# Attention and gated feed-forward in one kernel: norm statistics on half the columns, a finer weave in the first batch, and an earlier load

## The chip, the cores and the metric

The kernel runs on one core of a Trainium2 chip. The metric is the device time of one execution in microseconds (us), taken as the median of several runs. The engines named below are TensorE (PE in the profile; its weight loads are PEld), VectorE (DVE), ScalarE (ACT), GpSimd (POOL) and SyncE (SP); the last two issue most of the transfers (DMAs).

## The reference

There are 8 batches, 12 heads, 448 tokens and 64 numbers per head; the feed-forward has 768 inputs (12 x 64) and 1536 hidden units.

```python
scores = q @ k.T / sqrt(64)                    # per batch and head, 448 x 448
attn   = maximum(scores, 0)**2 / 448
x      = attn @ v                              # heads side by side: 3584 tokens x 768
rms    = sqrt(mean(x*x, axis=-1) + 1e-6)       # one number for each token
xn     = x / rms * rms_g
g, val = xn @ w_gate, xn @ w_val
out    = (g / (1 + exp(-g)) * val) @ w_out     # 3584 x 768, float32
```

## The kernel before

Everything is kept transposed: features on the partitions, a batch's 448 tokens along the columns. `xT` holds the attention's output of a batch as 6 blocks of 128 features (two heads each), `xD` the same with the halves of the partitions exchanged, made by four `swap` DMAs on SP's queue (L292). With both, each gate and value product contracts over 64 rows at a time, and two matmuls run side by side on the upper and lower rows. One round of `rounds` (L447) is such a pair, for gate (`psG`) and for value (`psV`); a block of 128 hidden units takes 12 rounds, the first 6 on `xT`, the last 6 on `xD`. Then ACT takes the silu of `psG` (L499) and DVE multiplies it by `psV` (L501) into `hT`. `outproj` (L505) multiplies `hT` by `w_out`, and ACT copies the result (`psO`) out (L521) for the stores (L532).

The order of instructions on every engine is the order in which the Python code emits them. `weave(main, sides)` emits a list of main units (half blocks of gate work, then output tiles), and ahead of main unit n every side step whose position is at most n. The side steps of batch b's gate are the attention of batch b+1. `along(p0, gap, fns)` gives such positions.

Attention of a pair of heads in batch 1 (`attention_second`, L326): `pe_transposes` turns k and q by TensorE into `psT`, and ACT or DVE copies them to `qkT`; a visit, `pair_scores` (L190), makes the scores of one of four groups of keys with two matmuls into `psS`, and ACT (L207), or DVE for the fourth group (L205), takes the relu; `squares` (L240, multiplying at L246) runs on DVE; `values` emits `attend` (L251, 16 matmuls into `psAV`) and `leave` (L275), in which ACT makes two blocks of `xT` (L284) and the squares `x2` (L285). `psS` and `psAV` share two buffers (pool `ps_s`); `psT`, `psG`, `psV`, `psO` share four (pool `ps_m`, tag "mm"). A matmul into a buffer waits until its former content has been read.

Batch 0 comes first, its attention alone (`attention_first`). Then the first EB = 3 blocks of batch 0's gate run on the raw `xT` and `xD`, before the norm is known, into `psE`; `early_out` copies them (L467), and `early_scale` (L473, DVE) and `early_rest` (L480 on ACT, L482 on DVE) finish them later. The other nine blocks of batch 0, with the attention of batch 1 woven in (`attention_second`; four of its steps have been taken by then), are the stage that the diff touches at the end: L652 to L658. From batch 2 on attention is `attention(b)` (L353), on halves of transposes made by DMA (`transposes`, L146, on SP; `fill`, L163, on GpSimd).

`norm_stat(b)` makes 1/rms of a batch: a matrix of ones, times the squares `x2`, gives every partition the sum over features (`psSS`); ACT takes the root, a further small ACT instruction brings back the table of silu, and DVE takes the reciprocal (`rstd`), which `norm_apply` (L425) multiplies onto `xT` block by block (L435), with a `swap` after three blocks and after six. For batches 0, 1 and 7 it takes 12 matmuls of 448 columns. For batches 2 to 6 `norm_stat_split` takes 6: the lower partitions get the sum of the even blocks and the upper ones that of the odd blocks, which a copy and an addition then bring together. For batch 1 it is emitted ahead of the first output tile, later after the first half of one.

GpSimd's queue loads in the order of emission (L582 to L607): batch 0, slices 0 and 1 of the gate and value weights (256 hidden units each), q and k of batch 1 in halves of six heads, slices 2 and 3, v of batch 1, slices 4 and 5, then `w_out`. `fetch(b)` loads a later batch.

Of the kernel before, what the change touches and what calls it, by code (L numbers as in the profile page):

```python
# [8 lines left out]
FP32 = mybir.dt.float32  # L9
BF16 = mybir.dt.bfloat16  # L10
ALU = mybir.AluOpType
ACT = mybir.ActivationFunctionType
# [22 lines left out]
def kernel(  # L35
# [20 lines left out]
    eps = 1e-6  # L56
    inv_attn = 1.0 / (float(D) * float(S))
    NT = 2 * S // P
    HALF = P // 2

    ctx.enter_context(tc.manual_schedule())

# [21 lines left out]
    def alloc_ld(b):  # L84
        for nm in ("q", "k", "v"):
            ld[nm, b] = ldpool.tile([PC, H, NCH * D], BF16, name=nm + "b", tag=nm + "b", bufs=2)
# [153 lines left out]
    def squares(b, j, cs, split=False):  # L240
        r = raw.pop((b, j, cs[0]))
        if split:
            nc.scalar.activation(out=r[:, 0], in_=r[:, 0], func=ACT.Square)
            nc.vector.tensor_tensor(out=r[:, 1], in0=r[:, 1], in1=r[:, 1], op=ALU.mult)
        else:
            nc.vector.tensor_tensor(out=r[:], in0=r[:], in1=r[:], op=ALU.mult)  # L246
        for i, c in enumerate(cs):
            for hh in range(2):
                rsq[b, 2 * j + hh, c] = r[:, i, hh, :]
# [76 lines left out]
    def attention_second(b):  # L326

        steps = []

        def visit(j, c):  # L330
            pair_scores(b, j, c, c == 3 and j > 0)
            if c == 0 and j:
                squares(b, j - 1, (2, 3))
            if c == 2:
                squares(b, j, (0, 1))

        def values(j):
            attend(b, (j, j + 1))
            leave(b, (j, j + 1))

        for j in range(HP):
            for c in range(NCH):
                steps.append(lambda j=j, c=c: visit(j, c))
                if c == 3 and j + 2 < HP:
                    steps.append(lambda j=j: pe_transposes(b, j + 2))
                if c == 3 and j in (2, 4):
                    steps.append(lambda j=j: values(j - 2))
        steps.append(lambda: squares(b, HP - 1, (2, 3)))
        steps.append(lambda: None)
        steps.append(lambda: values(HP - 2))  # L350
        return steps
# [29 lines left out]
    def halves(ps, w, lhsT, rhs, start, stop):  # L381

        for hf in range(2):
            prt = slice(hf * HALF, (hf + 1) * HALF)
            nc.tensor.matmul(out=ps[prt, :w], lhsT=lhsT[:, prt], rhs=rhs, start=start, stop=stop)  # L385

    def norm_stat(b):
        if 1 < b < B - 1:
            return norm_stat_split(b)
        psSS = ps_s.tile([P, 2, 512], FP32, name="psSS", tag="psS")[:, 0, :S]  # L390
        rstd = npool.tile([P, S], FP32, name="rstd", tag="rstd")
        for kt in range(KT):
            halves(psSS, S, ones_bf, x2s[b][:, kt, :], kt == 0, kt == KT - 1)
        nc.scalar.activation(
            out=rstd[:], in_=psSS[:], func=ACT.Sqrt, scale=1.0 / float(DM), bias=eps_col[:]
        )
        nc.scalar.activation(out=warm_act[:], in_=eps_col[:], func=ACT.Silu)
        nc.vector.reciprocal(out=rstd[:], in_=rstd[:])
        rstds[b] = rstd

    def norm_stat_split(b):


        psSS = ps_m.tile([P, S], FP32, name="psSS", tag="mm")
        rstd = npool.tile([P, S], FP32, name="rstd", tag="rstd")
        for i in range(KT // 2):
            for hf in (0, 1):
                prt = slice(HALF * hf, HALF * (hf + 1))
                nc.tensor.matmul(
                    out=psSS[prt, :], lhsT=ones_bf[:, prt], rhs=x2s[b][:, 2 * i + hf, :],  # L410
                    start=(i == 0), stop=(i == KT // 2 - 1),
                )
        low, high = slice(0, HALF), slice(HALF, P)
        nc.scalar.copy(out=rstd[low, :], in_=psSS[high, :])
        nc.vector.tensor_tensor(out=rstd[low, :], in0=psSS[low, :], in1=rstd[low, :], op=ALU.add)
        for prt in (high, low):
            nc.scalar.activation(
                out=rstd[prt, :], in_=rstd[low, :], func=ACT.Sqrt, scale=1.0 / float(DM),
                bias=eps_col[prt, :],
            )  # L420
        nc.scalar.activation(out=warm_act[:], in_=eps_col[:], func=ACT.Silu)
        nc.vector.reciprocal(out=rstd[:], in_=rstd[:])
        rstds[b] = rstd

    def norm_apply(b):  # L425
# [21 lines left out]
    def rounds(b, fb, parts, r0, r1, x=None):  # L447

        for r in range(r0, r1):
            kt, own = r % KT, r < KT  # L450
            src = (x or (xTs[b], xDs[b]))[0 if own else 1]
            for part in range(2):
                prt = slice(part * HALF, (part + 1) * HALF)
                h = 2 * kt + (part if own else 1 - part)
                nc.tensor.matmul(  # L455
                    out=parts[part][:, :S],
                    lhsT=wgv_sb[prt, h, fb * P : (fb + 1) * P],
                    rhs=src[prt, kt, :],
                    start=(r == 0),
                    stop=(r == 2 * KT - 1),  # L460
                )
# [24 lines left out]
    early = {}  # L486
    gvs = {}

    def block_first(b, fb):
        gvs[b, fb] = [  # L490
            ps_m.tile([P, S], FP32, name=nm, tag="mm")[:] for nm in ("psG", "psV")
        ]
        rounds(b, fb, gvs[b, fb], 0, KT)

    def block_second(b, fb):
        psG, psV = gvs.pop((b, fb))
        rounds(b, fb, (psG, psV), KT, 2 * KT)
        s = spool.tile([P, S], BF16, name="sil", tag="sil")
        nc.scalar.activation(out=s[:], in_=psG, func=ACT.Silu)  # L499
        hT, o = hidden(b)  # L500
        nc.vector.tensor_tensor(out=hT[:, fb, o : o + S], in0=s[:], in1=psV, op=ALU.mult)  # L501
# [33 lines left out]
            )  # L535
            g, k = g + n, k + 1

    def gate_value(b, f0=0):
        units = []
        for fb in range(f0, FT):  # L540
            units.append(lambda fb=fb: block_first(b, fb))
            units.append(lambda fb=fb: block_second(b, fb))
        if b < B:
            units[1], units[2] = units[2], units[1]
        return units

    def out_tiles(i, t0, t1):
# [41 lines left out]
    def warm(n):  # L589

        ps = ps_m.tile([P, S], FP32, name="psW", tag="mm")
        for _ in range(n):
            nc.tensor.matmul(out=ps[:], lhsT=warm_in[:, :P], rhs=warm_in[:], start=True, stop=True)  # L593

    for s in range(2):
        fetch_gv(s)
    alloc_ld(1)
    for h0 in (0, HH):
        load("q", 1, h0, h0 + HH)
        load("k", 1, h0, h0 + HH)  # L600
    for s in range(2, 4):
        fetch_gv(s)
    load("v", 1)
# [11 lines left out]
    with tc.tile_pool(name="qkT", bufs=2, side="right") as tp, tc.tile_pool(  # L615
        name="early", bufs=EB, side="right"
    ) as ep:
        late["qkT"], late["early"] = tp, ep
        warm(12)
        steps = attention_second(1)  # L620
        first = attention_first(0)
        for n, fn in enumerate(first):
            if n == len(first) - 3:
                pe_transposes(1, 0)
            if n == len(first) - 1:
                pe_transposes(1, 1)
            fn()
            if n % 3 == 2:
                warm(2)
        def early_block(fb):  # L630
            return [ps_m.tile([P, S], FP32, name="psE", tag="mm")[:] for _ in range(2)]

        raw_x = xTs[0], xDs[0]
        blocks = [early_block(fb) for fb in range(2)]
        near, far = KT + 4, 2 * KT
        norm_stat(0)
        rounds(0, 0, blocks[0], 0, KT, raw_x)
        rounds(0, 1, blocks[1], 0, KT, raw_x)
        for fb in range(2):
            steps.pop(0)()  # L640
            rounds(0, fb, blocks[fb], KT, near, raw_x)
        norm_apply(0)
        for fb in range(2):
            rounds(0, fb, blocks[fb], near, far, raw_x)
            early_out(0, fb, blocks[fb])
        for fb in range(2, EB):
            blocks.append(early_block(fb))
            for r0 in range(0, far, KT):
                steps.pop(0)()
                rounds(0, fb, blocks[fb], r0, r0 + KT, raw_x)  # L650
            early_out(0, fb, blocks[fb])
        main = gate_value(0, EB)  # L652
        sides = along(3.2, 1, [lambda fb=fb: early_scale(0, fb) for fb in range(EB)])
        sides += along(5.2, 1, [lambda fb=fb: early_rest(0, fb) for fb in range(EB)])
        sides += along(0, (len(main) - 1) / len(steps), steps)
        sides += [(9.1, lambda: fetch(2))]
        sides += [(14, lambda: trans_fill(2, 0)), (16, lambda: trans_fill(2, 1))]
        weave(main, sides)  # L658
    late["ost"] = pool("ostage", 3)

# [55 lines left out]
```

## Time and profile before

| | us |
|---|---|
| median of 12 runs (455.62 to 457.57) | 456.75 |
| the profiled execution | 456.38 |
| its span, first to last instruction | 454.6 |
| PE busy | 441.5 (97%) |
| ACT busy | 285.5 (63%) |
| DVE busy | 271.9 (60%) |
| DMA on GpSimd's queue, share of 16 engines | 41.9% |
| granted TensorE clock | 0.999 |

A row of a group or of the timeline gives line, engine, operation, result <- operands, form (partitions x columns) and count; in the timeline the start and the duration stand ahead, and in brackets behind stands how long the engine had been idle and what ended that. In a group's row the busy time, the mean duration of one in nanoseconds and the idle time before it follow. A row of the windows gives, for a stretch of time, its length, the busy time of PE, PEld, DVE, ACT and POOL (number of instructions in brackets), the clock, the DMA engines' share and GB/s. The ends of matmuls are modelled, so a busy PE is not a PE at its peak.

### The profile page before, as it was taken

How to read it: one execution, taken by the hardware profiler on the slowest of the kernel's cores; microseconds unless marked ns; L12 is line 12 of the kernel's file. 1: busy time of each engine (PE TensorE's matmuls, PEld its weight loads, DVE VectorE, ACT ScalarE, POOL GpSimd, SP SyncE). 2: the span in 40 equal slices, each digit the busy share in tenths (PEclk: the TensorE clock that was granted, in tenths of full speed). 3: DMA queues.
4: the chain of work that ended last, by engine and by line, in shares of the span. 5: the costliest groups of instructions: out<-in, count | busy, mean ns of one | idle time of the engine just before them, and what ended most of it. 6: DMA issues, size and time to landing. Idle time of an engine off the chain costs nothing.

```text
span 454.6 us, 10811 instructions
## 1 busy us (share of the span) xinstructions
PE 441.5 (97%) x4718; PEld 248.0 (55%) x4718; DVE 271.9 (60%) x326; ACT 285.5 (63%) x425; POOL 53.5 (12%) x79
## 2 busy tenths in 40 slices
PE   7999989999999999999999999999999999999996
PEld 3444444755556555555556555655556555565664
DVE  4979885637746666376656566386755466452210
ACT  4888786567766676676757577576757576542221
POOL 8333210400000300003000300003000000000000
PEclk9999999999999999999999999999999999999999
DMA  9999999997004998069913998059911910041013
GB/s 135 200 207 204 200 205 157 180 266 128 1 1 114 182 194 80 1 147 196 158 32 74 198 195 101 1 126 200 175 32 39 211 45 1 1 120 47 1 37 106
DMA packets 86672, 53.44 MB, mean 118 GB/s; under 512 B 36576, under 2 KB 80480, under 8 KB 86624
## 3 DMA queue, kind: packets, MB, share of 16 engines
q0 software_dynamic: 44496, 27.50, 41.9%
q1 hardware_dynamic: 41632, 24.67, 28.2%
q8 instruction: 37, 0.61, 0.5%
q10 hardware_dynamic: 496, 0.57, 0.4%
q14 instruction: 11, 0.09, 0.1%
HBM read 47.19 MB, written 11.01 MB: 128 GB/s over the span
## 4 chain that ended last, share of the span: by engine, by line
PE 84%; ACT 6%; DMA 4%; DVE 3%; issue 1%; SPq 1%; DVEq 0%
PE psG L455 35%; PE psO L385 20%; PE psV L455 9%; PE psAV L263 8%; PE psS L218 6%; DMA xD<-xT 4%; PE psW L593 2%; ACT r L187 1%; DVE xT L435 1%; PE psS L177 1%; ACT r L207 1%; PE psT L134 1%; SPq L292 1%; ACT xT L284 1%; ACT x L285 1%
## 5 line engine op out<-in xcount | busy, mean ns | idle before, releaser
L455 PEld LDWEIGHTS <-wgv_sb 64*128 64x128 bf16 x2304 | 122.0, 94 | 97.5 <-issue 10.4
L455 PE MATMUL psV<-xD,wgv_sb 64*128 64x448 bf16 x558 | 120.6, 349 | 0.9 <-DMA xD<-xT 0.8
L455 PE MATMUL psG<-xD,wgv_sb 64*128 64x448 bf16 x558 | 120.8, 349 | 0.0
L455 PE MATMUL psG<-xT,wgv_sb 64*128 64x448 bf16 x558 | 120.6, 349 | 0.0
L455 PE MATMUL psV<-xT,wgv_sb 64*128 64x448 bf16 x558 | 120.4, 349 | 0.0
L501 DVE TENSOR_TENSOR hT<-sil,psV 128x448 bf16<-128x448 bf16 x93 | 57.6, 619 | 104.9 <-ACT sil L499 103.9
L385 PE MATMUL psO<-wo_sb,hT 128*64 128x512 bf16 (+1 forms) x1344 | 113.5, 326 | 0.0
L232 ACT ACTIVATE r<-psS 112x896 bf16<-112x896 f32 x108 | 96.2, 918 | 22.7 <-PE psS L218 22.7
L385 PEld LDWEIGHTS <-hT 128*64 128x64 bf16 x1344 | 74.9, 110 | 36.2 <-issue 4.1
L499 ACT ACTIVATE sil<-psG 128x448 bf16<-128x448 f32 x93 | 50.7, 545 | 59.0 <-PE psV L455 38.9
L236 DVE TENSOR_TENSOR r<-r 112x1792 bf16<-112x1792 bf16 x72 | 78.3, 1089 | 4.9 <-ACT r L232 3.9
L521 ACT COPY ost<-psO 128x512 f32<-128x512 f32 (+1 forms) x54 | 25.2, 482 | 39.3 <-PE psO L385 35.0
L218 PE MATMUL psS<-qT,kT 64*128 64x448 bf16 (+1 forms) x288 | 47.8, 351 | 0.3 <-DVE r L230 0.3
L284 ACT ACTIVATE xT<-psAV,ga_sb 128x448 bf16<-128x448 f32 x47 | 27.5, 631 | 26.4 <-PE psAV L263 26.4
L230 DVE TENSOR_SCALAR r<-psS 112x896 bf16<-112x896 f32 x36 | 39.0, 1083 | 5.0 <-PE psS L218 5.0
L263 PE MATMUL psAV<-r,vb 112*64 112x448 bf16 x384 | 41.5, 356 | 0.0
L165 POOL DMA_DIRECT2D qT<-qT x12 | 6.5, 539 | 272.1 <-PE psS L218 143.8
L263 PEld LDWEIGHTS <-vb 112*64 112x64 bf16 x384 | 19.5, 109 | 19.8 <-issue 8.7
L218 PEld LDWEIGHTS <-kT 64*128 64x128 bf16 (+1 forms) x288 | 17.2, 96 | 19.3 <-issue 8.2
L435 DVE TENSOR_TENSOR xT<-xT,rstd 128x448 bf16<-128x448 bf16 x48 | 26.4, 619 | 0.3
L246 DVE TENSOR_TENSOR r<-r 112x1792 bf16<-112x1792 bf16 x23 | 24.4, 1084 | 1.3 <-ACT r L207 1.2
L285 ACT ACTIVATE x<-psAV 128x896 bf16<-128x896 f32 (+1 forms) x27 | 22.6, 836 | 0.8 <-DVE xT L280 0.8
(65 smaller groups left out, 254.7 us busy)
## 6 DMA issues: line engine op xcount, KB each, us to landing
vb<-in_v_dram POOLq DMA_DIRECT2D x7, 672.0 KB, 18.6
xD<-xT SPq DMA_DIRECT2D x28, 168.0 KB, 2.7
qb<-in_q_dram POOLq DMA_DIRECT2D x6, 672.0 KB, 12.4
kb<-in_k_dram POOLq DMA_DIRECT2D x6, 672.0 KB, 15.4
qT<-qT POOLq DMA_DIRECT2D x24, 168.0 KB, 3.7
out_dram<-ost SPq DMA_DIRECT2D x7, 336.0 KB, 5.8
wgv_sb<-in_moe_w_gate_dram POOLq DMA_DIRECT2D x6, 384.0 KB, 16.4
wgv_sb<-in_moe_w_val_dram POOLq DMA_DIRECT2D x6, 384.0 KB, 17.2
```

Of the source, the lines that this page charges most:

```text
L218: nc.tensor.matmul(out=psS[: end - o, hf, :S], lhsT=flat[prt, o:end], rhs=qT[prt, 1 - hf : 3 - hf, h % HH], start=True, stop=True,)
L230: nc.vector.tensor_relu(out=r[:, cp], in_=src)
L232: nc.scalar.activation(out=r[:, cp], in_=src, func=ACT.Relu)
L236: nc.vector.tensor_tensor(out=r[:], in0=r[:], in1=r[:], op=ALU.mult)
L263: nc.tensor.matmul(out=part[hh * D : (hh + 1) * D, :], lhsT=ld["v", b][:, 2 * j + hh, c * D : (c + 1) * D], rhs=rsq[b, 2 * j + hh, c], sta ...
L284: nc.scalar.mul(out=xTs[b][:, j, :], in_=psAV[:, i, :], mul=ga_sb[:, j : j + 1])
L285: nc.scalar.activation(out=x2s[b][:, js[0] : js[-1] + 1, :], in_=psAV, func=ACT.Square, scale=inv_attn)
L385: nc.tensor.matmul(out=ps[prt, :w], lhsT=lhsT[:, prt], rhs=rhs, start=start, stop=stop)
L435: nc.vector.tensor_tensor(out=x[:, kt, :], in0=raw_x[:, kt, :], in1=rstds[b][:], op=ALU.mult)
L455: nc.tensor.matmul(out=parts[part][:, :S], lhsT=wgv_sb[prt, h, fb * P : (fb + 1) * P], rhs=src[prt, kt, :], start=(r == 0), stop=(r == 2 * ...
L499: nc.scalar.activation(out=s[:], in_=psG, func=ACT.Silu)
L501: nc.vector.tensor_tensor(out=hT[:, fb, o : o + S], in0=s[:], in1=psV, op=ALU.mult)
```

## The change

Three things are changed together.

1. `norm_stat` is one function for all batches. The sums of the first 224 tokens are made on the lower 64 partitions and those of the last 224 on the upper 64 (12 matmuls of 224 columns, six pairs). Root and reciprocal work on 128 x 224. Then four copies of 64 x 224 spread the result over all partitions: DVE copies each half to its own partitions, ACT each half to the other ones.
2. In the first batch's gate stage a main unit is 3 rounds and not 6 (`gate_value(0, EB, KT // 2)`), with all positions doubled; the order of the rounds is the same. An empty step follows each of the two first `values` of `attention_second`.
3. The first halves of batch 1's q and k are loaded between the first and the second weight slice.

```diff
@@ attention_second
                 if c == 3 and j in (2, 4):
                     steps.append(lambda j=j: values(j - 2))
+                    steps.append(lambda: None)
@@ norm_stat
     def norm_stat(b):
         if 1 < b < B - 1:
-            return norm_stat_split(b)
-        psSS = ps_s.tile([P, 2, 512], FP32, name="psSS", tag="psS")[:, 0, :S]
+            psSS = ps_m.tile([P, S], FP32, name="psSS", tag="mm")[:, :W]
+        else:
+            psSS = ps_s.tile([P, 2, 512], FP32, name="psSS", tag="psS")[:, 0, :W]
+        half = npool.tile([P, W], FP32, name="rhalf", tag="rhalf")
         rstd = npool.tile([P, S], FP32, name="rstd", tag="rstd")
         for kt in range(KT):
-            halves(psSS, S, ones_bf, x2s[b][:, kt, :], kt == 0, kt == KT - 1)
...
             for hf in (0, 1):
                 prt = slice(HALF * hf, HALF * (hf + 1))
                 nc.tensor.matmul(
-                    out=psSS[prt, :], lhsT=ones_bf[:, prt], rhs=x2s[b][:, 2 * i + hf, :],
-                    start=(i == 0), stop=(i == KT // 2 - 1),
+                    out=psSS[prt, :], lhsT=ones_bf[:, prt],
+                    rhs=x2s[b][:, kt, hf * W : (hf + 1) * W],
+                    start=(kt == 0), stop=(kt == KT - 1),
                 )
...
+        nc.scalar.activation(
+            out=half[:], in_=psSS, func=ACT.Sqrt, scale=1.0 / float(DM), bias=eps_col[:]
+        )
         nc.scalar.activation(out=warm_act[:], in_=eps_col[:], func=ACT.Silu)
-        nc.vector.reciprocal(out=rstd[:], in_=rstd[:])
+        nc.vector.reciprocal(out=half[:], in_=half[:])
+        for own in (True, False):
+            for hf in (0, 1):
+                src = slice(HALF * hf, HALF * (hf + 1))
+                dst = src if own else slice(HALF * (1 - hf), HALF * (2 - hf))
+                o = rstd[dst, hf * W : (hf + 1) * W]
+                if own:
+                    nc.vector.tensor_copy(out=o, in_=half[src, :])
+                else:
+                    nc.scalar.copy(out=o, in_=half[src, :])
         rstds[b] = rstd
@@ block_first and block_second become block_part; gate_value
-    def gate_value(b, f0=0):
+    def gate_value(b, f0=0, n=KT):
         units = []
         for fb in range(f0, FT):
-            units.append(lambda fb=fb: block_first(b, fb))
-            units.append(lambda fb=fb: block_second(b, fb))
-        if b < B:
-            units[1], units[2] = units[2], units[1]
+            for r in range(0, 2 * KT, n):
+                units.append(lambda fb=fb, r=r: block_part(b, fb, r, r + n))
+        m = KT // n
+        units[m : 2 * m], units[2 * m : 3 * m] = units[2 * m : 3 * m], units[m : 2 * m]
         return units
@@ the loads
+    alloc_ld(1)
     for s in range(2):
         fetch_gv(s)
-    alloc_ld(1)
-    for h0 in (0, HH):
-        load("q", 1, h0, h0 + HH)
-        load("k", 1, h0, h0 + HH)
+        load("q", 1, s * HH, (s + 1) * HH)
+        load("k", 1, s * HH, (s + 1) * HH)
@@ the first batch's gate stage
-        main = gate_value(0, EB)
-        sides = along(3.2, 1, [lambda fb=fb: early_scale(0, fb) for fb in range(EB)])
-        sides += along(5.2, 1, [lambda fb=fb: early_rest(0, fb) for fb in range(EB)])
+        main = gate_value(0, EB, KT // 2)
+        sides = along(6.4, 2, [lambda fb=fb: early_scale(0, fb) for fb in range(EB)])
+        sides += along(10.4, 2, [lambda fb=fb: early_rest(0, fb) for fb in range(EB)])
         sides += along(0, (len(main) - 1) / len(steps), steps)
-        sides += [(9.1, lambda: fetch(2))]
-        sides += [(14, lambda: trans_fill(2, 0)), (16, lambda: trans_fill(2, 1))]
+        sides += [(18.2, lambda: fetch(2))]
+        sides += [(28, lambda: trans_fill(2, 0)), (32, lambda: trans_fill(2, 1))]
         weave(main, sides)
```

More of the change, by code (lines that the diff above doesn't have):

```diff
@@ L58 @@
     NT = 2 * S // P
-    HALF = P // 2
+    HALF, W = P // 2, S // 2
     ctx.enter_context(tc.manual_schedule())
@@ L388, in norm_stat @@
         if 1 < b < B - 1:
-            return norm_stat_split(b)
-        psSS = ps_s.tile([P, 2, 512], FP32, name="psSS", tag="psS")[:, 0, :S]
+            psSS = ps_m.tile([P, S], FP32, name="psSS", tag="mm")[:, :W]
+        else:
+            psSS = ps_s.tile([P, 2, 512], FP32, name="psSS", tag="psS")[:, 0, :W]
+        half = npool.tile([P, W], FP32, name="rhalf", tag="rhalf")
         rstd = npool.tile([P, S], FP32, name="rstd", tag="rstd")
         for kt in range(KT):
-            halves(psSS, S, ones_bf, x2s[b][:, kt, :], kt == 0, kt == KT - 1)
[L394 to L406, printed above, removed]
             for hf in (0, 1):
@@ L409, in norm_stat_split @@
                 nc.tensor.matmul(
-                    out=psSS[prt, :], lhsT=ones_bf[:, prt], rhs=x2s[b][:, 2 * i + hf, :],
-                    start=(i == 0), stop=(i == KT // 2 - 1),
-                )
[L413 to L420, printed above, removed]
-        nc.scalar.activation(out=warm_act[:], in_=eps_col[:], func=ACT.Silu)
-        nc.vector.reciprocal(out=rstd[:], in_=rstd[:])
+                    out=psSS[prt, :], lhsT=ones_bf[:, prt],
+                    rhs=x2s[b][:, kt, hf * W : (hf + 1) * W],
+                    start=(kt == 0), stop=(kt == KT - 1),
+                )
+        nc.scalar.activation(
+            out=half[:], in_=psSS, func=ACT.Sqrt, scale=1.0 / float(DM), bias=eps_col[:]
+        )
+        nc.scalar.activation(out=warm_act[:], in_=eps_col[:], func=ACT.Silu)
+        nc.vector.reciprocal(out=half[:], in_=half[:])
[8 more added lines that the diff above has]
+                    nc.scalar.copy(out=o, in_=half[src, :])
         rstds[b] = rstd
@@ L487, with block_part @@
     gvs = {}
[L489 to L495, printed above, removed]
+    def block_part(b, fb, r0, r1):
+        if r0 == 0:
+            gvs[b, fb] = [
+                ps_m.tile([P, S], FP32, name=nm, tag="mm")[:] for nm in ("psG", "psV")
+            ]
+        rounds(b, fb, gvs[b, fb], r0, r1)
+        if r1 < 2 * KT:
+            return
         psG, psV = gvs.pop((b, fb))
-        rounds(b, fb, (psG, psV), KT, 2 * KT)
         s = spool.tile([P, S], BF16, name="sil", tag="sil")
```

## Prediction

> **What bounds the kernel now.** I read the page first, then the windows by stage, then the timeline of TensorE, then the waits.
>
> ```profile
> span 454.6 us, 10811 instructions
> PE 441.5 (97%) x4718; PEld 248.0 (55%) x4718; DVE 271.9 (60%) x326; ACT 285.5 (63%) x425; POOL 53.5 (12%) x79
> ```
>
> TensorE is busy 97% of the span at full clock, so only less matmul work or fewer stalls of TensorE shorten it. But 97% flatters: the timeline lists a 448-column matmul at 0.35 us while the next pair (two matmuls side by side on the halves of the array) starts 0.19 us later, so each listed idle time hides a further 0.16 us or so. I therefore measure a stall from start to start, less 0.19. The stages:
>
> ```profile
> 0.00:32.50 32.50, 28.61 (x268) 12.20 (x268) 24.52 (x33) 22.46 (x32) 17.37 (x29) 1.00 1.27 179
> 43.20:79.00 35.80, 32.86 (x360) 16.88 (x356) 27.67 (x33) 26.75 (x41) 5.63 (x7) 1.00 1.35 187
> 79.00:92.00 13.00, 13.00 (x158) 9.63 (x156) 6.87 (x8) 7.02 (x11) 4.98 (x7) 1.00 1.15 185
> 92.00:106.00 14.00, 12.87 (x130) 7.14 (x129) 7.96 (x10) 9.47 (x13) 0.00 (x0) 1.00 1.14 229
> 204.00:392.00 188.00, 188.00 (x2009) 106.24 (x2003) 119.72 (x140) 125.64 (x186) 15.99 (x23) 1.00 0.64 109
> ```
>
> (PE, PEld, DVE, ACT, POOL, clock, DMA share, GB/s.) From 204 to 392 us there is nothing to win. The loss sits where batch 1's attention is woven into batch 0's gate (43-79), and in the first visit to batch 1's gate (92-106). The timeline shows who ends those stalls:
>
> ```profile
> 48.33 0.39 PE L134 MATMUL psT<-ident,kb 112*64 112x112 bf16 x8 [0.74 <-ACT sil L499]
> 58.52 0.76 PE L197 MATMUL psS<-qkT 64*128 64x448 bf16 x4 [0.43 <-DVE r L205]
> 61.42 0.37 PE L197 MATMUL psS<-qkT 64*128 64x448 bf16 x2 [0.82 <-ACT r L207]
> 71.40 0.36 PE L197 MATMUL psS<-qkT 64*128 64x448 bf16 x2 [0.42 <-ACT x L285]
> 73.45 0.36 PE L197 MATMUL psS<-qkT 64*128 64x448 bf16 x2 [0.36 <-ACT r L207]
> 95.62 0.35 PE L455 MATMUL psV<-xD,wgv_sb 64*128 64x448 bf16 x1 [0.57 <-DMA xD<-xT]
> 96.66 0.35 PE L455 MATMUL psV<-xD,wgv_sb 64*128 64x448 bf16 x1 [0.22 <-DMA xD<-xT]
> 104.86 0.36 PE L218 MATMUL psS<-qT,kT 64*128 64x448 bf16 x2 [0.35 <-DVE r L230]
> ```
>
> Start to start these cost 0.90, 0.59, 1.00, 0.58, 0.54, then 0.87 and 0.48, then 0.53. With three smaller ones (0.29 before the psAV at 55.14, 0.21 at 58.91, 0.35 at 69.48) the woven stage loses about 4.5 us to late evacuations, and the swap 1.35.
>
> **Part 1, the finer weave and the empty steps.** Before, a unit of gate work is 6 rounds (1.13 us) and 29 steps are laid over 18 units, 17/29 = 0.59 apart. Positions round up to whole units, so visits fall in twos: both of visit(3,0) and (3,1) before unit 8, a unit after values(0). After, a unit is 3 rounds (0.57 us) and 31 steps lie 35/31 = 1.13 units apart: never two before one unit, and an empty step follows each of the two first `values`. No operation is added; the cost of the edit itself is nothing.
>
> What it is worth is counted by hand from the rows: relu 0.92 us (0.81 back to back), silu 0.55, `leave` 2.0. After values(0), ACT runs `leave` until 2.0 us past the attend; visits now ask for psS at 1.13, 1.89, 2.65, 3.97 instead of two and two. The second waits 0.1 for the psAV buffer, the third some 0.55 for the relu of the first; the rest fit: 0.7 against 1.80 (0.59+0.21+1.00). After values(2): some 0.3 against 1.47 (0.58+0.54+0.35). The relu of visit(2,3) on DVE (57.38, the releaser at 58.52) stands behind early_scale 2 and early_rest 0 (1.08+0.62) in DVE's order; its position 10.16 now lies ahead of theirs (10.4), so it is 1.6 us earlier. Transpose 3 still comes right after block 3, waiting for silu: 0.7 against 0.90. Sum: 1.1+1.17+0.2 = 2.5.
>
> Against it: ACT is busy 26.75 of the 35.8 us and TensorE needs about 30 (35.8 less 6 of stalls and small changeover gaps). A group of three ACT visits, one silu and one qkT copy is 3x0.81+0.45+0.8 = 3.7 us of ACT beside 4 visits, 4.5 units and a transpose of TensorE, 0.76+2.6+0.5 = 3.9. So there is little slack. Ends: a loss of 2.4 (0.35 for each of 20 visits, 7 us, in place of 4.5) and a gain of 3.3. I take 2.2.
>
> **Part 2, the statistics.** TensorE, batches 0, 1, 7: six pairs of 448 columns (1.14 at 396.52) become six of 224. Nearest row: 24 psO matmuls of 256 columns in 1.43 us (chain, 147.20), 0.119 a pair against 0.107 by columns; so 224 costs 0.095 to 0.119, six 0.57-0.71. Batch 7 gains 0.43-0.57 in full. Batch 1 gains 0.05: the last pair waits for `leave` (ACT x ends at 79.8) however short it is. Batch 0 gains nothing: TensorE then waits for xD (landings 38.52, 39.19). Batches 2-6 had three pairs of 448 (0.57) and get six of 224: 0 to +0.14 each; I take 0.07, 0.35 in all. Net gain 0.1 (-0.2 to +0.6).
>
> The chain behind it, with the rows:
>
> ```profile
> L422 DVE RECIPROCAL rstd<-rstd 128x448 f32<-128x448 f32 x5 | 14.8, 2952 | 10.3 <-ACT rstd L417 10.3
> L398 DVE RECIPROCAL rstd<-rstd 128x448 f32<-128x448 f32 x3 | 8.9, 2953 | 8.5 <-ACT rstd L394 8.5
> L394 ACT ACTIVATE rstd<-psSS,eps_col 128x448 f32<-128x448 f32 x3 | 1.9, 635 | 0.9 <-PE psSS L385 0.9
> ```
>
> Sqrt on 224: ACT copies of 256 and 128 columns (373, 267) give 0.83 ns a column, so 635-186 = 0.45. Four copies: on ACT 0.35 each by the same rows, two overlapped 0.65; on DVE 0.2-0.4 each, ending no later. ACT's copies queue behind the silu table load (1.28+0.2), which covers the reciprocal (1.5); if that cover failed, they and the psO copies behind them would wait, bounded by psO's four buffers of 1.3-2.6 us.
>
> [...] Chain, batch 1: 0.635+2.95 to 0.45+1.5+0.65 = 1.0 saved. Batches 2-6: 188.53 to 194.73 is 6.2 (copy, table load, two roots of 0.67, reciprocal); now 1.28+0.45+1.5+0.65 = 3.9: 2.3 saved.
>
> Where it counts: only where xD is late. Batch 2 loses 0.35 at 202.36 (380 ns with its pair): gone, 0.3. Batches 3-7 show no such stall: nothing.
>
> Batch 1's swap was issued at 86.95-89.14 and landed at 93.78-96.62, 7 us, in a crowd with the fetch of batch 3 (POOL, 84.81-88.91). TensorE moves 2.2 earlier and the chain 1.0 more, while that crowd does not move: it hangs on fills behind transposes that wait for loads (q landed 70.48, k 73.93) at 187 GB/s. SP's transposes are issued until 83.27, so the swaps go at about 83.7-85.9, mostly ahead of the crowd. Ends: SP's transposes delay them and they still take 7 us (gain 0.3), or both stalls and the DVE echo at 104.86 vanish (1.9). I take 1.6.
>
> **Part 3, the loads.** Batch 1's first q and k halves overtake the second weight slice: k lands at about 25.7 instead of 30.35, removing a wait of 0.2-0.37 at 30.39. The slice lands at 30.4 instead of 27.2 and is first used at 39.8: hidden by 9 us. But the next bound is xD at 38.5-39.2, hung on batch 0's last `leave` and SP: I take 0.1 (0 to 0.4).
>
> **Sum:** 2.2+0.1+0.3+1.6+0.1 = 4.3. The profiled execution took 456.38 (span 454.6, 1.8 around it), 0.4 below the median 456.75. So span 450.3, that run 452.1, median 452.5.
>
> **The rivals.** (a) ACT is the real bound of the weave: stalls shift from psS to others, 0.7 won, and SP's transposes hold the swap, 0.8: total 2.0, 454.8. For: ACT's 3.7 against 3.9. (b) No change: the weave redistributes its stalls and the swap's landing follows the DMA crowd; 0.5 won, 456.3. For: the swap already took 7 us. (c) Slower: with even spacing and two psS buffers every third visit meets two unreleased ones, since ACT (0.81-0.92 a relu, with silu and `leave` between) is slower than the 0.76 us between visits; each wait ends a block later, its silu queues later still, and the swap gains only half (0.8). With 0.8+0.5 from elsewhere the kernel breaks even at 0.29 us per visit (20 visits: 5.8 against 4.5+1.3), is measurably slower from 0.34, and at 0.40 (8.0) loses 2.2: 459.0. Against: two visits at once is the worse placing for two buffers, and DVE takes every fourth. (d) More: stalls nearly gone, 6.2 won, 450.5.
>
> **How the numbers follow.** This kernel's measurement tells 0.2% (0.9 us) from no change: 455.85 to 457.65 is "same". Chances: 4.3 won 0.42, (a) 0.22, (b) 0.10, (c) 0.14, (d) 0.12. Faster 0.76, same 0.10, slower 0.14. The range runs from (d) to (b), 450.5 to 456.3, leaving out the slower cases and the far ends.
>
> **What would show it.** Right: psS waits on ACT r, DVE r and ACT x below 2.5 us in batch 0's gate; no TensorE wait on xD near 92; RECIPROCAL at 1.5 us; psSS x12 of 224 columns in 0.6-0.7; steady stages of unchanged length. Wrong: gate stage of batch 0 still 35 us or longer, swaps landing 7 us after issue, 224-column pairs well above 0.12, or ACT waiting on the reciprocal.

## The result, and the profile after

The changed kernel took 453.45 us in the median (12 runs, 452.25 to 455.84) against 456.72 before (49 runs): a ratio of 0.9936, 95% interval 0.9925 to 0.9947, 2.9 us faster. The prediction was 452.5, that is 4.3 us faster, in a range of 450.5 to 456.3. (All ratios leave out runs more than 1.5% above the fastest of their kernel, which is one run of swap_first_split.) The profiled execution's span is 451.2, 3.4 less than before, and this is what the steps below divide. The page:

```profile
span 451.2 us, 10901 instructions
PE 440.0 (98%) x4748; PEld 248.4 (55%) x4748; DVE 262.0 (58%) x337; ACT 283.1 (63%) x431; POOL 53.6 (12%) x79
```

TensorE has 1.5 us less of listed busy time; the rest of the 3.4 us is idle time. The windows begin at the same events as those of before (start of batch 0's gate, of batch 1's sums, of batch 1's gate); the last two end at the same times:

```profile
43.10:77.20 34.10, 32.74 (x358) 17.11 (x355) 25.87 (x31) 26.74 (x40) 5.63 (x7) 1.00 1.35 195
77.20:90.00 12.80, 12.49 (x158) 9.47 (x156) 6.02 (x10) 7.50 (x13) 4.95 (x7) 1.00 1.13 195
90.00:106.00 16.00, 15.43 (x157) 8.39 (x156) 10.66 (x13) 11.04 (x15) 0.00 (x0) 1.00 1.10 210
204.00:392.00 188.00, 188.00 (x2022) 106.51 (x2020) 113.39 (x140) 123.19 (x186) 12.06 (x18) 1.00 0.60 102
```

The woven stage now lasts 34.1 us where it lasted 35.8, with ACT busy for the same 26.7: TensorE waits less, ACT does not work less. (DVE's 25.9 in place of 27.7 comes with two instructions fewer in the window.) The times of the same TensorE events in the two profiles divide the gain:

| from one event to the next | gain, us |
|---|---|
| start to the first gate block of batch 0 | 0.14 |
| to the first matmul of batch 1's sums (the weave) | 1.65 |
| batch 1's sums | 0.19 |
| batch 1's gate, with its wait on the swap | 0.73 |
| batch 3's gate | 0.24 |
| batch 7's sums | 0.56 |
| elsewhere (sums of batches 2 to 6: -0.01 each) | -0.14 |
| span | 3.37 |

The waits of TensorE in the woven stage before (us in total, times, longest), as the profile lists them:

```profile
PE psS L197 <- ACT r L207: 1.2, 2, 0.8
PE psT L134 <- ACT sil L499: 0.7, 1, 0.7
PE psS L197 <- DVE r L205: 0.4, 1, 0.4
PE psS L197 <- ACT x L285: 0.4, 1, 0.4
```

And after, those of the whole span without the ones of batch 0's attention and of the warm-up:

```profile
PE psE L451 <- DMA xD<-xT: 0.8, 3, 0.4
PE psT L134 <- ACT sil L495: 0.6, 1, 0.6
PE psS L218 <- DVE r L230: 0.3, 1, 0.3
PE psS L197 <- ACT r L207: 0.3, 1, 0.3
PE psAV L263 <- DVE r L246: 0.3, 1, 0.3
PE psSS L400 <- ACT x L285: 0.3, 1, 0.3
PE psV L451 <- DMA xD<-xT: 0.2, 1, 0.2
```

Of the woven stage's waits, psS on DVE r and on ACT x are gone and psS on ACT r fell from 1.2 to 0.3. Two are new, at the stage's end: psAV on the last squares and psSS on the last `leave`. The wait of psE on xD in batch 0 grew from 0.6 to 0.8: shorter sums only bring TensorE sooner to a transfer that lands when it did (its last two parts at 38.51 and 39.05 us, before at 38.52 and 39.19). Batch 1's swap still waits, 0.2 listed, 0.55 from start to start. The new statistics (by form):

```profile
L409 DVE RECIPROCAL rhalf<-rhalf 128x224 f32<-128x224 f32 x8 | 12.4, 1553 | 34.6 <-ACT rhalf L405 34.6
L400 PE MATMUL psSS<-x,ones_bf 128*64 128x224 bf16 x96 | 6.2, 260 | 0.3 <-ACT x L285 0.3
L418 ACT COPY rstd<-rhalf 64x224 f32<-64x224 f32 x16 | 6.0, 377 | 0.9
L416 DVE COPY rstd<-rhalf 64x224 f32<-64x224 f32 x16 | 4.3, 272 | 0.4
```

The reciprocal nearly halved, 2.95 to 1.55: a straight line through these two sizes gives 6.2 ns a column and 0.15 us besides (an estimate from the two rows, 2952 and 1553 ns). And the chain of work at batch 1's swap:

```profile
79.75 0.46 ACT rhalf L405
80.23 1.56 DVE rhalf L409
81.82 0.38 ACT rstd L418
82.21 0.39 ACT rstd L418
82.61 3.31 DVE xT L431 x6
86.45 7.40 DMA xD<-xT
```

All steps up to the swap are about as long as forecast; the DMA is not. It still takes 7.4 us and ends in TensorE's wait.

### The profile page after: what moved, and what is told of

Read it like the earlier page. It is cut to its first block, busy times and chain, and to the rows that moved or that the text cites. A ratio compares the mean times of both kernels' runs of the same rounds, so it can differ in the third digit from the quotient of the medians.

```text
span 451.2 us, 10901 instructions
## 1 busy us (share of the span) xinstructions
PE 440.0 (98%) x4748; PEld 248.4 (55%) x4748; DVE 262.0 (58%) x337; ACT 283.1 (63%) x431; POOL 53.6 (12%) x79
## 3 DMA queue, kind: packets, MB, share of 16 engines
q1 hardware_dynamic: 41632, 24.67, 26.7%
## 4 chain that ended last, share of the span: by engine, by line
PE 87%; ACT 4%; DVE 3%; DMA 3%; issue 1%; SPq 1%; DVEq 0%; ACTq 0%
PE psG L451 37%; PE psO L386 22%; PE psAV L263 8%; PE psV L451 8%; PE psS L218 7%; DMA xD<-xT 3%; PE psW L589 2%; ACT r L187 1%; PE psS L177 1%; PE psT L134 1%; ACT xT L284 1%; PE psSS L400 1%; DVE xT L431 1%; PE psS L197 1%; PE psE L451 1%
## 5 line engine op out<-in xcount | busy, mean ns | idle before, releaser
L409 DVE RECIPROCAL rhalf<-rhalf 128x224 f32<-128x224 f32 x8 | 12.4, 1553 | 34.6 <-ACT rhalf L405 34.6
```

## The experiments

Theory: the finer units of the weave carry most of it; the statistics give the matmuls of batch 7 and the shorter chain, the latter only at batch 1's swap; the loads give nothing. Rivals: the empty steps, or the load order, or the statistics in batch 0, are what lifts the woven stage. "By event" is read off the profiles as in the table; ratios are against the kernel before on the same chip.

**weave_only:** the kernel before with the finer units, the doubled positions and the empty steps.

> The kernel before with part 1 alone (units of 3 rounds, the empty steps). Theory: the woven stage gains by itself what the two profiles show there, 1.65 us up to the start of batch 1's sums; TensorE then meets batch 1's swap with the old 3.6 us chain and the same crowd of transfers, so it gives back up to 0.5: 1.2 to 1.7 us faster. Rival A (the stage gains because the earlier norm of batch 0 frees VectorE, or because of the load): under 0.7. Rival B (every part is worth only with the others): no change.

454.45 us, ratio 0.9951 (0.9932 to 0.9970): 2.2 faster. By event the stage gained 1.74, as in the whole change, and 0.39 was given back at batch 1's gate, where its two stalls on xD became 1.19 and 0.54. The 2.2 lies above the expected 1.2 to 1.7, with an interval that reaches into it; rivals A and B fall.

**stat_only:** the kernel before with the new `norm_stat`.

> The kernel before with part 2 alone (sums of 224 columns, root and reciprocal on half the columns, four copies). Theory: 0.56 us at batch 7 from the matmuls, 0.25 at batch 2's swap, 0.2 at batch 1's sums, and 0.3 to 0.9 at batch 1's swap, where the chain is 1.0 shorter: 1.3 to 1.9 faster. Rival A: the copies and small instructions cost what the reciprocal gains, 0.3 to 0.6 faster, from the matmuls of batch 7 alone. Rival B: the earlier norm of batch 0 also lifts the woven stage, then 2 or more.

455.23, ratio 0.9983 (0.9967 to 0.9999): 0.8 faster. By event 0.56 at batch 7's sums, 0.19 at batch 1's, 0.24 at batch 1's gate, 0.24 at batch 3's, and 0.00 in the woven stage (rival B falls). It lies between the theory and rival A: the matmuls are certain, and the chain gave a quarter of a microsecond at batch 1: the swaps, issued behind the fetch of batch 3, landed 7.4 to 8.2 us after their issue.

**load_only:** the kernel before with the new order of the loads.

> The kernel before with part 3 alone (first halves of batch 1's q and k ahead of the second weight slice). Theory: removes a wait of 0.2 to 0.4 us at 30.4, after which xD bounds the stage: 0 to 0.2 faster, within what can be told from no change. Rival: it is the load order that brings all transfers of batch 2 forward by about a microsecond and with them the swap of batch 1: 0.5 to 1.0 faster, with k of batch 2 landing at 73.2 and not 73.9.

456.70, ratio 1.0003 (0.9988 to 1.0018): no difference. The rival falls.

**empty_only:** the kernel before with the two empty steps alone.

```diff
                 if c == 3 and j in (2, 4):
                     steps.append(lambda j=j: values(j - 2))
+                    steps.append(lambda: None)
```

> The kernel before with the two empty steps alone, units of 6 rounds as before: positions 17/31 = 0.55 apart. Theory (the finer units separate the visits, the empty steps only give room after leave): the pairs of visits remain, a gain of 0.2 to 0.7. Rival (the gain of the weave is the room after leave): 1.2 or more, about as much as part 1 in whole. If two visits now fall ahead of units where they did not before: slower by up to 0.5.

457.72, ratio 1.0028 (1.0015 to 1.0042): 1.3 slower. Both the theory's gain and the rival's are refuted; even the loss was larger than allowed for. Its waits in the woven stage:

```profile
PE psS L197 <- ACT r L207: 2.1, 5, 0.9
PE psS L197 <- ACT x L285: 1.3, 2, 0.6
```

Two more steps in the same 18 units bring the positions from 0.59 to 0.55 units apart; worked out from the positions, eight units have two visits ahead of them where six had. psS waits on ACT 3.4 us where it was 1.6 before (1.2 and 0.4). The stage grew by 1.43.

**fine_no_empty:** the changed kernel without the empty steps.

> The changed kernel without the two empty steps (29 steps over the 36 finer units, 1.21 apart). The empty steps alone with coarse units cost 1.4 us. Theory: the finer units carry the gain of part 1 and the empty steps give little with them: within 0.5 of the changed kernel, so 2.3 to 3.1 under the kernel before. Rival (the empty step is what gives ACT room after leave, and needs the finer units to be of use): 1 or more lost, 1.0 to 2.0 under the kernel before, with stalls of psS ended by ACT x and ACT r back behind each values.

454.15, ratio 0.9946 (0.9933 to 0.9960), 2.5 under before, where the changed kernel was 2.9: the intervals overlap, so the times do not separate the theory from the rival. The profile does. It is 1.6 above the changed kernel's, 0.95 of it in the stage, which gains 0.70 over before and not 1.65. The second psS after each `values` loses 0.8 (from start to start, less 0.19) to ACT's squares in `leave` (changed: 0.2 and nothing):

```profile
PE psS L197 <- ACT x L285: 1.3, 2, 0.6
PE psS L197 <- ACT r L207: 0.3, 1, 0.3
```

These are the stalls that the rival named. In the stage the finer units alone give 0.70, the empty steps alone cost 1.43, and both together give 1.65: the room after `leave` is worth 0.95, but only where the units are fine. That the finer units carry most of the gain, as the theory had it, is not borne out. (A single profile is good evidence here: the stage's gain was 1.65 in all five profiles with the new statistics and part 1 as it is, and 1.74 in both with the old statistics.)

**turn_later:** the changed kernel, each later transpose one visit later.

```diff
-                if c == 3 and j + 2 < HP:
-                    steps.append(lambda j=j: pe_transposes(b, j + 2))
+                if c == 0 and j and j + 1 < HP:
+                    steps.append(lambda j=j: pe_transposes(b, j + 1))
```

> The changed kernel with each later transpose by TensorE one visit later, so that psT no longer follows the end of block 3. Theory: the stall of 0.84 us at 48.09, which the prediction left at 0.7, is psT waiting for the silu of block 3; it goes: 0.4 to 0.9 faster than the changed kernel (3.3 to 3.8 under before). Rival: ACT is what bounds the stage, the stall moves to the next psS or psAV: within 0.3 of the changed kernel.

454.06, ratio 0.9939 (0.9928 to 0.9951): as the changed kernel. The rival's size was right, though the stall moved to a psV and not to psS or psAV, within the four buffers of `ps_m`:

```profile
PE psV L451 <- ACT qkT L141: 1.7, 2, 1.0
```

psT no longer waits for the silu, but the next block's psV waits for ACT to copy psT away, 1.7 in place of 0.6.

**swap_first:** the changed kernel, batch 1's swap on GpSimd's queue, where the fetch of batch 3 stands behind it.

```diff
-                    swap(b, kt - 2, kt + 1)
+                    swap(b, kt - 2, kt + 1, nc.gpsimd if b == 1 else None)
```

> The changed kernel with batch 1's swap issued on the queue of GpSimd, where the fetch of batch 3 then stands behind it. Theory: the swap takes 7 us because it shares the DMA engines with that fetch; ahead of it, it lands 3 to 4 us after its issue, the wait of 0.55 at 93.89 goes, and perhaps the 0.70 at 102.15 behind it: 0.5 to 1.2 faster than the changed kernel (3.4 to 4.1 under before). Rival (the swap is slow by itself, or the stores and transposes slow it): still 6 us or more, no gain, and the fetch comes later for nothing.

451.74 (4 runs), ratio 0.9892 (0.9878 to 0.9906): 4.9 under before, 2.0 under the changed kernel by the ratios, more than the theory's 0.5 to 1.2. Landing times from issue, in the DMA issues between 84 and 92 us, first of the changed kernel and then of this one:

```profile
xD<-xT SPq DMA_DIRECT2D x4, 168.0 KB, 7.1
```
```profile
xD<-xT POOLq DMA_DIRECT2D x4, 168.0 KB, 5.3
```

They land at 88.2 to 91.9, and TensorE waits for none. The fetch of q, behind them, lands at 99.4 in place of 94.3 and nothing waits for it. This is what the prediction had counted on and the change itself did not reliably bring. The run changes two things at once, the swap's queue and its place ahead of the fetch, and does not separate them.

Of the 1.5 us between the two profiles 0.43 lies at batch 1's gate and 0.5 at the start, which varies from run to run. The other 0.6 lies at the very end and is not a gain of the earlier swap: from the issue of the last store to the end of the span it is 3.2 us in all four profiles with the moved swap and 3.8 in the other ten, while that store lands in 2.1 in all of them. What grows shorter is the row of semaphore waits on SP behind it (1.65 us from the landing to the end, now 1.06); why moving four transfers to another queue does that, no run shows. It is the fastest version found (swap_first_split cannot be told from it), and beats both kernels.

**root_again:** the changed kernel with a second reciprocal (1.55 us) whose result is not used.

```diff
+        again = npool.tile([P, W], FP32, name="again", tag="again")
+        nc.vector.reciprocal(out=again[:], in_=half[:])
         nc.vector.reciprocal(out=half[:], in_=half[:])
```

> The changed kernel with a second reciprocal of 224 columns, whose result is not used, ahead of the real one: each batch's chain is 1.55 us longer, more than the change saved at batch 1 (1.0). Theory: the chain's length is worth something only at batch 1's swap and perhaps at batch 3's: 0.3 to 1.6 slower than the changed kernel. Rival (the shorter chain gives nothing, the statistics' gain is that of the matmuls alone): within 0.3 of the changed kernel. Rival (the chain counts in each batch): 3 or more slower.

455.58, ratio 0.9993 (0.9969 to 1.0017): 2.6 slower than the changed kernel by the ratios, above the theory's range and short of "in each batch". Three of its 12 runs took 457.65 to 460.78 at a granted clock of 0.992 to 0.995, and the profiled one, with a span of 458.9, is of these. TensorE and its clock at batch 1's swap:

```profile
95.43 0.35 PE L453 MATMUL psV<-xD,wgv_sb 64*128 64x448 bf16 x1 [2.08 <-DMA xD<-xT]
96.37 0.53 PE L453 MATMUL psG<-xD,wgv_sb 64*128 64x448 bf16 x1 [0.22 <-DMA xD<-xT]
98.71 0.53 PE L453 MATMUL psV<-xD,wgv_sb 64*128 64x448 bf16 x1 [1.81 <-DMA xD<-xT]
```
```profile
92.00:96.40 4.40, 2.10 (x21) 0.73 (x16) 0.00 (x0) 1.74 (x2) 0.54 (x1) 1.00 1.26 248
96.40:98.70 2.30, 0.50 (x1) 0.08 (x1) 0.00 (x0) 0.00 (x0) 0.00 (x0) 0.50 1.26 249
98.70:103.00 4.30, 4.29 (x24) 2.06 (x25) 1.70 (x3) 2.00 (x3) 0.00 (x0) 0.50 1.31 265
```

After waits of 2.08 and 0.22 the clock falls to 0.50 at 96.4. The wait of 1.81 comes when it has fallen, and until 103 pairs start 0.37 apart, not 0.19. At batch 1's gate this profile is 6.8 us behind the changed kernel's, for a chain that is 1.55 longer; most of it is waiting for xD, whose last part landed 9.2 us after its issue. Beyond batch 1's gate the batches up to 6 take the same time as in the changed kernel (0.13 in all), and before batch 0's gate 0.3 more, so in this profile the chain counts at batch 1 almost alone. The other nine runs, at a clock of 0.998 or more, took 455.24 to 455.82, still some 1.6 above what the changed kernel's ratio gives on this chip (453.9); where they lose it, no profile shows.

**changed_again:** the changed kernel on the chip of the next three.

> The changed kernel once more, beside the next three on one chip, as their yardstick: 2.4 to 3.4 under the kernel before.

453.32, ratio 0.9946 (0.9920 to 0.9972): as before. Its profile gains the same 1.65 in the woven stage, but at batch 1's gate it is 0.23 slower than the kernel before, where the first profile of the same kernel gained 0.73:

```profile
93.59 0.35 PE L451 MATMUL psG<-xD,wgv_sb 64*128 64x448 bf16 x1 [0.73 <-DMA xD<-xT]
94.24 0.35 PE L451 MATMUL psV<-xD,wgv_sb 64*128 64x448 bf16 x1 [0.31 <-DMA xD<-xT]
```

The swaps were issued at 83.77 to 85.84, the first ahead of the fetch of q (84.24), yet the last two landed 8.2 and 8.4 us after their issue. turn_later gained 0.69 at batch 1's gate and fine_no_empty 0.40. So the gain of 0.73 there is one draw among -0.2 to 0.7. What the profiles show beside it is the landing of the last swap, 7.40 us after its issue in the first and 8.4 in this one; that its meeting with the fetch sets it is the author's reading. The next three runs, with the swap ahead in the fetch's queue, gain 0.76 to 1.28.

**swap_first_split:** swap_first, the last squares of batch 1 shared by ACT and DVE.

```diff
-        steps.append(lambda: squares(b, HP - 1, (2, 3)))
+        steps.append(lambda: squares(b, HP - 1, (2, 3), True))
```

> The changed kernel with batch 1's swap on GpSimd's queue ahead of the fetch, and the last squares of batch 1 shared by ACT and VectorE. Theory: the stall of psAV on DVE r at 75.1 (0.54 to 0.67) goes, but ACT's square (0.95) stands ahead of leave and of the sums: 0 to 0.5 faster than swap_first, 4.6 to 5.6 under before. Rival (ACT bounds the end of this stage): 0.2 to 0.9 slower than swap_first.

452.53 (5 runs), ratio 0.9911 (0.9887 to 0.9936). In its profile the wait of psAV is gone and batch 1's sums begin 0.53 sooner relative to the first gate block, but 0.40 is lost again at batch 1's gate, where the last swap landed at 92.7. The ratio does not separate it from swap_first; inconclusive.

**swap_first_root_again:** swap_first with the second reciprocal.

> swap_first with the second, unused reciprocal (chain 1.55 us longer in each batch), which cost 2.1 to 2.6 with the swap in the crowd. Theory: the chain has about 1 us of slack once the swap does not share with the fetch, so 0.3 to 1.0 is lost, and no run with a reduced clock is left. Rival (the chain counts by itself, crowd or not): 1.5 or more lost, as before.

453.38, ratio 0.9939 (0.9916 to 0.9962): 2.1 slower than swap_first by the ratios, against the theory's 0.3 to 1.0 and within the rival's 1.5 or more. The profile, 2.9 above swap_first's, shows where: 2.3 before batch 0's gate, 0.00 from there to batch 2's sums, batch 1's swap included, and 0.5 behind batch 7's sums. So at batch 1 the chain has its slack, as the theory said, and the loss is at places it had not thought of, the start above all, again by the clock:

```profile
37.00:40.00 3.00, 1.59 (x11) 0.56 (x10) 2.88 (x7) 2.67 (x5) 0.75 (x1) 1.00 1.41 208
40.00:43.30 3.30, 3.30 (x21) 1.62 (x18) 3.30 (x7) 2.11 (x5) 1.43 (x2) 0.50 1.48 198
```

TensorE waited three times for xD before 39.5 (0.53, 0.41, 0.47), and at 40.0 the clock fell; the forecast that no run with a reduced clock would be left was wrong. Two of its 7 runs have a mean clock of 0.996. The other five have 0.999 or more and are still 1.0 to 2.5 above swap_first's median, which was taken on another chip; where those lose it, no profile shows.

**swap_first_old_stat:** swap_first with the statistics of the kernel before.

> swap_first with the statistics of the kernel before (longer chain: 1.0 at batch 1, 2.3 at batches 2 to 6; 448 columns in batches 0, 1 and 7). Theory: what remains of the statistics' worth is the matmuls, 0.56 at batch 7 and 0.2 at batch 1, for the chain is hidden: 0.6 to 1.1 slower than swap_first, 4.0 to 4.5 under before. Rival (the shorter chain still counts): 1.5 or more slower than swap_first.

453.19, ratio 0.9927 (0.9904 to 0.9949): 1.6 slower than swap_first by the ratios, with intervals that hold both forecasts. Between the profiles (1.2 in all) 0.56 is at batch 7's sums, 0.19 at batch 1's, -0.12 at batch 1's gate, and 0.65 before batch 0's gate. For the chain at batch 1 the profile sides with the theory: with the swap ahead of the fetch the long chain, too, is hidden there.

## Why the prediction was right, and where its terms were off

- **The weave, 2.2 forecast, 1.65 to 1.74 shown.** The mechanism is the one given, in both its halves: visits no longer in twos, and an empty step behind `values`. From start to start, less 0.19, the stalls after the first `values` are 0.75 (0.7 forecast), after the second 0.14 (0.3), at transpose 3 0.80 (0.7). Not in the sum was psAV's stall of 0.49 at 75.43: the last squares stand behind the relu of visit(5,3) in DVE's order. (The 0.29 at 55.14 in the prediction's 4.5 is a start-to-start time without the 0.19 taken off, so 0.1.) Moving the relu of visit(2,3) ahead in DVE's order was not needed: in fine_no_empty its position, 10.86, lies behind 10.4 as before, and psS does not wait for DVE there. The price of the empty steps, "nothing", held only with the finer units: alone they cost 1.3.
- **The matmuls.** Batch 7: 0.56, at the top of 0.43 to 0.57. Batch 1: 0.19, not 0.05: the last pairs do wait for `leave`, but only two short ones come after it. Batches 2 to 6: +0.01 each, not +0.07. So the net gain was 0.7 where 0.1 was forecast, just beyond that term's own range. The row of 24 matmuls in 1.43 was read as 0.119 a pair. In the trace pairs of 256 columns start 0.109 apart; in that row's group the rest lies at its ends (0.13 from the first pair to the second, 0.21 from the last to the gate's first). Pairs of 224 start 0.0955 apart, half of the 0.19 of 448.
- **The chain.** 0.45, 1.55 and 0.77 against 0.45, 1.5 and 0.65. No run made ahead of the change shows the 1.5 for a reciprocal of 224 columns; the changed kernel's row shows 1553 ns, where 448 columns took 2952.
- **Batch 1's swap, 1.6 forecast, 0.73 shown in one profile and -0.23 in another of the same kernel.** The step that failed is "that crowd does not move". The fetch of batch 3 was issued at 83.57 in place of 84.81 and the swaps at 84.38 to 86.45, so fetch and swap met again; the last landed 7.4 us after its issue, which the prediction had named as a sign of being wrong. The "DVE echo" at 104.86 was no echo of the swap: the same stall stands at 102.15 after the change, and at 101.25 in swap_first (0.35 listed each time), where TensorE waits for no xD at all.
- **The stall at 202.36** lies at batch 3's gate; the prediction called it batch 2's. It shrank by 0.24 in all nine profiles with the new statistics. With the old ones it was 0.30, 0.26 and 0.10 shorter in weave_only, empty_only and swap_first_old_stat, and 0.34 longer in load_only. So it varies with the old chain and not with the new one; that the shorter chain removed it is likely, not shown.
- **The loads, 0.1 forecast:** nothing. k landed at 26.1 (25.7 forecast), the slice at 31.0 (30.4); TensorE then waited for xD at 38 to 39 as foreseen.
- **Rivals.** The slower one (breaking even at 0.29 for each visit) did not occur: the stage's psS waits are 0.3 in all. The size of (a)'s second half came, not its reason: SP's transposes were issued by 82.4 and the first swap at 84.38, as soon as DVE had made its blocks.
- **The sign on psS** (below 2.5 us) could not tell: the listed waits were 2.0 before already.

So the direction and the weave are understood. That the total fell only a third short of the forecast owes something to luck: the matmuls gave 0.6 more than their term, and the weave and the swap 0.55 and 0.9 less.

The three parts alone give 2.2 + 0.8 - 0.1 = 2.9, the whole 2.9: they add up within their intervals.

## What to carry to other kernels

Where side work is laid among units of a bound engine, make the units fine first: positions that round to the same unit put two claims on the same two buffers at once (the finer units alone gave the stage 0.70 us). Room in the right place then adds to it, here 0.95; with coarse units the same room made the stage 1.43 longer. A chain that is made shorter gains little for certain if it ends in a transfer that another, movable transfer meets; here it helped to put the urgent one ahead in the same queue (5.3 us to landing in the median, not 7.1). And read a group's time per instruction from start to start, not from its total.

## What the runs showed of the hardware

The granted clock halved in two profiles after waits none of which was longer than 2.1 us. From the start of the first wait to the fall TensorE was idle for 2.30 of 3.05 us in root_again (2.08 and 0.22) and for 1.41 of 2.7 in swap_first_root_again (0.53, 0.41, 0.47), with matmuls in between. The clock stayed at 0.50 for 6.8 us and for 3.4 us. Pairs of 448 columns then start 0.37 apart, which cost some 2.2 and 1.6 us on top of the waits (an estimate from 12 and 9 pairs, 0.18 each).

At the end of the span, where TensorE has no work left, the clock falls to 0.50 as well: 3.36 us after the last matmul in the changed kernel (446.79 to 450.14) and 3.70 after it in the kernel before (450.13 to 453.83). In the two profiles above no stretch that long was idle throughout, and the clock fell all the same. How much spread idle time goes with a fall, these runs do not settle: in the changed kernel TensorE is idle for 1.53 of the 3.64 us from 6.63 on (0.78 and 0.75), and the clock stays at 1.00.

Mean clocks of 0.996 or lower came in 14 of 77 runs of the kernels with the new statistics (9 of 58 without the two that have a second reciprocal) and in 3 of 97 of those with the old ones (the kernel before among them). That the shorter sums of batch 0, which leave TensorE longer waiting for xD (0.8 us in place of 0.6), do this in the runs without a profile is argued from swap_first_root_again and not shown. In the changed kernel's first 12 runs the two slowest, 455.38 and 455.84, are the two at 0.996.
